# A one-token attention block on one core: the last eight rounds written out step by step, and one inverse root seeded on ScalarE

## The chip, the cores and the metric

One core of a Trainium2 chip runs the kernel. The time is device microseconds (us) of one execution. The runs of the kernel before gave 393.55, 395.03 and 395.13 us, median 395.03.

## What is computed

Four rows (batch B = 4, one token each, 512 channels) pass through an attention over a cache of 4096 positions and a small mixer. Both are modulated by six vectors that come from `c`.

```python
mod = (_silu(c) @ w_mod).reshape(c.shape[0], 6, 1, -1)
sa, ca, ga, sb, cb, gb = (mod[:, 0], mod[:, 1], mod[:, 2], mod[:, 3], mod[:, 4], mod[:, 5])
h = _layernorm(x, axis=-1) * (1 + ca) + sa
x = x + ga * _A_ref(h, A_k_cache, A_v_cache, A_wq, A_wo)
h = _layernorm(x, axis=-1) * (1 + cb) + sb
x = x + gb * _B_ref(h, B_w1, B_b1, B_w2, B_b2)
...
        scores = jnp.einsum("bhqd,bhkd->bhqk", q, k) * (Dh ** -0.5)
        p = _softmax(scores, axis=-1)
        o = jnp.einsum("bhqk,bhkd->bhqd", p, v)
        return (lambda x, *d: x.transpose(*d))(o, 0, 2, 1, 3).reshape(B, Sq, Hq * Dh) @ wo
...
        u = jnp.einsum("bsd,sf->bdf", h, w1) + b1                  # (B, D, F)
        u = _gelu(u)
        y = jnp.einsum("bdf,fs->bds", u, w2) + b2                  # (B, D, S)
```

There are 32 query heads on 8 key/value heads of 128 channels, and F = 1792. The two caches are 64 loads of 2 MB of float32 each, and every byte of them is read once.

## The kernel before

The work is 32 **rounds**: round i is batch row i // 8 and key/value head i % 8. Below, K29 is the keys of round 29 and V29 its values, 2 MB each. Up to round 29 the keys of round i + 2 and the values of round i come in one 4 MB load (`load_pair`); the last loads are cut: K30, K31, V28, V29 in two pieces, V30 in two, V31 in four (1 MB, 512 KB, 256 KB, 256 KB, called V31a to V31d here), and then `wm5`, the last 1 MB of `w_mod`. All loads land in one ring of three 4 MB slots (tag "kv"), are issued on SP's queue in program order, and a load can be issued when the reads of its slot's former content are over.

The steps of a round i, with their engines:

- `scores(i)`: eight products of the query with K on PE into a PSUM tile s; then the row maximum m on DVE (L241).
- `colmax(i)`: PE turns m (tile pm, L247), DVE takes the maximum over four groups (L249).
- `expo(i)`: PE spreads the maximum over the partitions (pb, L256), DVE copies it (L258), ACT makes the exponentials p and their sums l (L261).
- `transposes(i)`: PE turns p (eight blocks, L268, written over s) and sums l (pl, L272); DVE copies the blocks (L276) and forms the scaled selector sel (L279, L281).
- `values(i)`: sixteen products with V on PE (pv, L292; for round 30 the tile is called pve), then a copy on DVE (po, L296). Round 31 has `values_last` (L302, L306).
- `project_a(i)` picks the heads (pt, PE L317) and copies them (oT, DVE L319); `project_b(i)` multiplies with `wo` (pa, or pq and pgx in the last batch row, PE L328 and L335) and adds up on DVE (L344). Rounds 30 and 31 add straight in PSUM, in pgx; `wo` of these two rounds is first multiplied by the gate, by `fold_gate` (L537).

Once a batch row has its eight rounds, a `Mixer` does the second half for it in pieces between the rounds of the next row: residual, layernorm, modulation, second layernorm, and then seven pairs of expand (DVE, L405), gelu (ACT, L448) and contract (PE, L410). Batch row 3 has nothing after it: `finish` does its second half alone at the end. There and in `adaln` the inverse root of a variance is made on DVE from an integer seed and two refining steps (`rsqrt`, L99 to L116).

The order on each engine is the order of the calls; `manual_schedule` is on and nothing is rearranged. Until round 27 one loop body is repeated (L548 to L588), in which each helper holds steps of several engines: `scores` stands whole ahead of `project_a`, `transposes`, `project_b`, `colmax`, `values`, `expo`. Rounds 28 to 31 are written out below it (L589 to L639). The PSUM tiles pm, pb, pl, pt, pq and pst share two buffers, so each of them waits until the last but one has been read.

Of the kernel before, what the change touches and what calls it, by code (L numbers as in the profile page):

```python
# [28 lines left out]


@with_exitstack
def adaln_decode(ctx: ExitStack, tc: tile.TileContext, small, x, wmod, wq, kk, kv, vv, wo, out):
# [20 lines left out]
    nc.sync.dma_start(sm, small)  # L53
# [177 lines left out]
    S, SEL, SP = {}, {}, {}  # L231

    def scores(i):
        b, h = divmod(i, HKV)
        s = ps_s.tile([P, 1024], F32, name=f"s{i}", tag="s")
        for n in range(2):
            for c in range(4):
                mm(s[32 * c:32 * c + 32, n * 512:(n + 1) * 512], QT[:, b, h, :],  # L238
                   KT[i][:, (n * 4 + c) * 512:(n * 4 + c + 1) * 512], start=True, stop=True)
# [12 lines left out]

    def expo(i):
        s, mx = S[i]
        pb = ps_m.tile([P, 1], F32, name="pb", tag="m")
        mm(pb, mx.rearrange("o c r -> o (c r)"), neg1, start=True, stop=True)  # L256
        nm = wk.tile([P, 1], F32, name="nm")
        dv.tensor_copy(nm, pb)  # L258
        p = wk.tile([P, 1024], F32, name="p", tag="p")
        l = wk.tile([P, 1], F32, name="l")  # L260
        nc.scalar.activation(p, s, AF.Exp, bias=nm, accum_out=l)  # L261
        S[i] = [s, p, l]

    def transposes(i, then=None):
        s, p, l = S.pop(i)
        pt = s.rearrange("p (k n) -> p k n", k=8)
        for k in range(8):
            nc.tensor.transpose(pt[:, k, :], p[:, k * P:(k + 1) * P], ident)  # L268
        if then:
            then()  # L270
        pl = ps_m.tile([P, 1], F32, name="pl", tag="m")
        mm(pl, grp, l, start=True, stop=True)  # L272
        if i == NS - 1:
            dv.tensor_copy(pTl[:, :, :, 0:REP], pt.rearrange("p k (c r) -> p k c r", c=4)[:, :, :, 0:REP])
        else:
            dv.tensor_copy(pTs[i % 3][:, :, 0:2 * REP].rearrange("p k (c r) -> p k c r", c=2),  # L276
                           pt.rearrange("p k (h c r) -> p (k h) c r", h=2, c=2)[:, :, :, 0:REP])
        rl = wk.tile([P, 1], F32, name="rl")
        dv.reciprocal(rl, pl)  # L279
# [4 lines left out]
    PV = {}  # L284

    def values(i, ks, pv=None):
        if ks[0] == 0:
            PV[i] = ps_v.tile([P, 2 * DH], F32, name="pv", tag="pv") if pv is None else pv
        pv = PV[i]
        for k in ks:  # L290
            q = k % 4
            mm(pv[32 * q:32 * q + 32, :], pTs[i % 3][:, k, :],  # L292
               VT[i][:, k * 2:(k + 1) * 2, :].rearrange("p j d -> p (j d)"), start=(k < 4), stop=(k >= 12))
        if ks[-1] == 15:
            po = wk.tile([P, 2 * DH], F32, name="po")
            dv.tensor_copy(po, pv)  # L296
            SP[i] = (SEL.pop(i), po)

    def values_last(i, ks, pv):
        for k in ks:  # L300
# [3 lines left out]
        if ks[-1] == 7:  # L304
            po = wk.tile([P, DH], F32, name="po")
            dv.tensor_copy(po, pv)  # L306
            SP[i] = (SEL.pop(i), po)

    ACC = {}
    OT = {}  # L310

    def project_a(i):
        sel, po = SP.pop(i)
        pt = ps_m.tile([P, REP], F32, name="pt", tag="m")
# [3 lines left out]
        oT = wk.tile([P, REP], F32, name="oT")  # L318
        dv.tensor_copy(oT, pt)  # L319
        OT[i] = oT  # L320

    def project_b(i, pa=None):
# [7 lines left out]
        else:  # L330
# [54 lines left out]

    def bcast(h1, b, pb=None):
# [7 lines left out]
    def affine(pst, pb):  # L394
# [5 lines left out]
        rsqrt(var, P, "e", out=wr, times=w1n)  # L400
# [18 lines left out]
    class Mixer:  # L419
# [254 lines left out]
```

## Time and profile before

| | |
|---|---|
| median of three runs | 395.03 us |
| profiled execution | 393.89 us, span 392.1 us, granted TensorE clock 0.908 |
| PE busy | 298.3 us (76%), 3180 instructions |
| DVE busy | 180.3 us (46%), 491 instructions |
| ACT busy | 99.6 us (25%), 123 instructions, among them 22 table loads of 1283 ns |
| SP's DMA queue | 157.33 MB, 93.6% of 16 engines' span |
| HBM | 401 GB/s over the span |

The span is the stretch from the first to the last instruction of the profiled execution; the other 1.8 us of its 393.89 lie around it. In the views, a row of the timeline gives start and duration in us, engine, line of the kernel, operation, tiles and count; the bracket says how long the engine was idle just before, and who released it. A float32 product shows as two MATMUL records. PEld is the weight load that goes with a product, SPq and DVEq are the queues ahead of SP and DVE.

### The profile page before, as it was taken

The numbers are of one execution on the slowest core, as the hardware profiler recorded it, in microseconds if no ns is written. First come the engines' busy times: TensorE is split into PE (matmuls) and PEld (weight loads), VectorE is DVE, ScalarE is ACT, GpSimd is POOL, SyncE is SP. The second block draws the span as 40 slices with busy tenths as digits, with TensorE's granted clock in tenths as the row PEclk, the third lists the DMA queues.
The fourth block names the chain that finished last, engine by engine and source line by source line (L and its number), as shares of the span: only waits on it lengthen the run. The fifth ranks groups of instructions, "written<-read, shape, count | busy, mean of one in ns | idle before, by whom it ended". The sixth has DMA issues, their size and how long they took to land.

```text
span 392.1 us, 7228 instructions
## 1 busy us (share of the span) xinstructions
PE 298.3 (76%) x3180; PEld 146.8 (37%) x3180; DVE 180.3 (46%) x491; ACT 99.6 (25%) x123; POOL 0.7 (0%) x6
## 2 busy tenths in 40 slices
PE   0578685913868739978698879998888879899885
PEld 0012142400533305434243325553334225555663
DVE  0620331510433404666365524765555356557766
ACT  1001120110110201114548111145751111465316
POOL 0000000000000000000000000000000000000000
PEclk9989886985998957999899976999999889999997
DMA  8999999999999999999999999999999999999600
GB/s 325 428 431 431 428 453 440 404 448 431 425 431 426 436 426 438 433 440 439 426 431 424 430 435 430 433 428 434 436 435 430 431 430 430 416 425 420 258 3 3
DMA packets 7415, 157.80 MB, mean 402 GB/s; under 512 B 964, under 2 KB 980, under 8 KB 1368
## 3 DMA queue, kind: packets, MB, share of 16 engines
q1 hardware_dynamic: 7376, 157.33, 93.6%
q8 instruction: 25, 0.41, 0.4%
q14 instruction: 6, 0.05, 0.0%
q10 hardware_dynamic: 8, 0.00, 0.0%
HBM read 157.32 MB, written 0.01 MB: 401 GB/s over the span
## 4 chain that ended last, share of the span: by engine, by line
DMA 64%; PE 27%; DVE 6%; ACT 1%; issue 1%; SPq 0%; DVEq 0%
DMA kv<-in_kv 57%; PE s L238 7%; DMA kv<-in_vv 5%; PE pv L292 3%; PE pa L328 3%; PE s L268 3%; PE s L137 2%; PE qs L152 2%; DMA sm<-in_small 2%; PE pt L317 2%; DVE mx L249 1%; PE py L410 1%; DVE acc L344 1%; PE pb L256 1%; PE pm L223 1%
## 5 line engine op out<-in xcount | busy, mean ns | idle before, releaser
L238 PE MATMUL s<-kv,QT 128*32 128x512 f32 x512 | 76.5, 725 | 55.0 <-DMA kv<-in_kv 54.6
L261 ACT ACTIVATE p<-s,nm 128x1024 f32<-128x1024 f32 x32 | 35.7, 1115 | 212.9 <-DVE nm L258 212.8
L241 DVE TENSOR_REDUCE m<-s 128x1 f32<-128x1024 f32 x32 | 39.2, 1225 | 104.9 <-PE s L238 104.8
L292 PE MATMUL pv<-kv,pT 128*32 128x256 f32 x960 | 64.5, 387 | 0.0
L238 PEld LDWEIGHTS s<-kv,QT 128*32 128x32 f32 x512 | 15.6, 123 | 94.8 <-DMA kv<-in_kv 62.4
L268 PE MATMUL s<-ident,p 128*128 128x128 f32 x256 | 36.5, 288 | 0.6 <-ACT p L261 0.6
L268 PEld LDWEIGHTS s<-ident,p 128*128 128x128 f32 x256 | 31.5, 157 | 3.7 <-ACT p L261 1.9
L292 PEld LDWEIGHTS pv<-kv,pT 128*32 128x32 f32 x960 | 25.6, 110 | 15.3 <-issue 0.6
L317 PEld LDWEIGHTS pt<-sel,po 128*128 128x128 f32 x126 | 17.6, 202 | 30.8 <-issue 25.7
L328 PE MATMUL pa<-wo,oT 128*32 128x512 f32 x192 | 27.3, 642 | 0.0
L249 DVE TENSOR_REDUCE mx<-pm 1x128 f32<-1x512 f32 x32 | 21.5, 672 | 0.7 <-PE pm L247 0.7
L317 PE MATMUL pt<-sel,po 128*128 128x4 f32 x126 | 20.3, 266 | 1.1 <-DVE po L296 1.0
L448 ACT ACTIVATE u<-u 128x1024 f32<-128x1024 f32 x20 | 20.3, 1051 | 2.2 <-DVE u L405 2.1
L405 DVE TENSOR_SCALAR u<-hb,wr,sm 128x512 f32<-128x512 f32 x40 | 19.9, 540 | 1.9 <-PE py L416 1.9
L137 PE MATMUL s<-wm,sT 128*4 128x512 f32 x16 | 9.6, 770 | 14.3 <-DVE sT L123 14.3
L344 DVE TENSOR_TENSOR acc<-acc,pa 128x512 f32<-128x512 f32 x21 | 14.5, 688 | 11.3 <-PE pa L328 11.3
L296 DVE COPY po<-pv 128x256 f32<-128x256 f32 x30 | 12.7, 423 | 11.8 <-PE pv L292 11.8
L261 ACT ACT_TABLE_LOAD x9 | 11.5, 1283 | 25.6 <-DVE nm L258 25.5
L256 PEld LDWEIGHTS pb<-neg,mx 1*128 1x128 f32 x64 | 9.4, 182 | 20.0 <-DVE mx L249 20.0
L256 PE MATMUL pb<-neg,mx 1*128 1x1 f32 x64 | 12.1, 256 | 5.9 <-DVE mx L249 5.9
L448 ACT ACT_TABLE_LOAD x11 | 14.1, 1283 | 0.2
L276 DVE COPY pT<-s 128x128 f32<-128x128 f32 x31 | 9.0, 291 | 9.9 <-PE s L268 9.2
(142 smaller groups left out, 231.1 us busy)
## 6 DMA issues: line engine op xcount, KB each, us to landing
kv<-in_kv SPq DMA_DIRECT2D x28, 4096.0 KB, 21.6
wq<-in_wq SPq DMA_DIRECT2D x2, 4096.0 KB, 16.3
wo<-in_wo SPq DMA_DIRECT2D x4, 2048.0 KB
kv<-in_kv SPq DMA_DIRECT2D x3, 2048.0 KB, 17.4
wm<-in_wmod SPq DMA_DIRECT2D x2, 2048.0 KB, 16.1
kv<-in_kk SPq DMA_DIRECT2D x1, 4096.0 KB
kv<-in_vv SPq DMA_DIRECT2D x3, 1024.0 KB
kv<-in_kv SPq DMA_DIRECT2D x2, 1024.0 KB, 17.6
```

Of the source, the lines that this page charges most:

```text
L238: mm(s[32 * c:32 * c + 32, n * 512:(n + 1) * 512], QT[:, b, h, :], KT[i][:, (n * 4 + c) * 512:(n * 4 + c + 1) * 512], start=True, stop=True)
L241: dv.tensor_reduce(m, s, axis=AX.X, op=OP.max)
L249: dv.tensor_reduce(mx, pm.rearrange("o (c r) -> o r c", c=4).unsqueeze(1).to_broadcast([1, 4, 32, 4]), axis=AX.X, op=OP.max)
L256: mm(pb, mx.rearrange("o c r -> o (c r)"), neg1, start=True, stop=True)
L261: nc.scalar.activation(p, s, AF.Exp, bias=nm, accum_out=l)
L268: nc.tensor.transpose(pt[:, k, :], p[:, k * P:(k + 1) * P], ident)
L292: mm(pv[32 * q:32 * q + 32, :], pTs[i % 3][:, k, :], VT[i][:, k * 2:(k + 1) * 2, :].rearrange("p j d -> p (j d)"), start=(k < 4), stop=(k ...
L317: mm(pt, po[:, c * DH:(c + 1) * DH], sel[:, c * REP:(c + 1) * REP], start=(c == 0), stop=(c == n - 1))
L328: mm(pa[32 * g:32 * g + 32, :], oT[:, g:g + 1].to_broadcast([P, 32]), wo_t[h][:, g, :], start=True, stop=True)
L344: dv.tensor_add(ACC[b], ACC[b], pa)
L405: dv.tensor_scalar(u[:, e, :], hb, wr[:, j:j + 1], b1[:, j:j + 1], op0=OP.mult, op1=OP.add)
L448: nc.scalar.activation(u, u, AF.Gelu_apprx_tanh)
```

## The change

Three things change.

1. **The helpers are split** into steps of one engine each (`scores`, `row_max`, `turn_max`, `col_max`, `spread_max`, `copy_max`, `expo`, `turn`, `sums`, `copy_p`, `scale`, `copy_v`, `pick`, `copy_o`, `project`, `add_up`; the mixer's `fold`, `gather`, `spread` likewise). The loop runs to round 23 in the old order. From the end of round 23 on a string lists the steps one by one, so that values can go in quarters and a step of one engine no longer brings the other engines' steps with it. V29 comes in one load and not in two.
2. **The last batch row's first inverse root** is seeded on ACT (`Abs_reciprocal_sqrt`) and refined once on DVE. Two small activations (T2, T3) load the table for it and then the gelu table again. The sign of the modulated row is turned by this, which `w1` in place of `w1n` takes back.
3. **The load of `small`** (128 rows of 236 bytes: w1, b1, w2, c, b2) is cut into rows 0 to 5, 6 to 15 and 16 to 127.

```diff
-    nc.sync.dma_start(sm, small)
+    for lo, hi in ((0, 6), (6, 16), (16, P)):
+        nc.sync.dma_start(sm[lo:hi], small[lo:hi])
...
+    def adaln_last(b, pst):
+        mean, var = norm(pst)
...
+        nc.scalar.activation(y, var, AF.Abs_reciprocal_sqrt, scale=1.0 / C2)
+        dv.scalar_tensor_tensor(a, XK[:, b], mean, prep[:, 3], op0=OP.subtract, op1=OP.mult)
+        dv.scalar_tensor_tensor(t, y, var, y, op0=OP.mult, op1=OP.mult)
+        dv.scalar_tensor_tensor(y, t, 3.0 * C2, y, op0=OP.subtract, op1=OP.mult)
+        dv.scalar_tensor_tensor(h1, a, y, prep[:, 2], op0=OP.mult, op1=OP.subtract)
+        return h1, stats(h1, b)
...
-    for i in range(NS - 4):
+    for i in range(NS - HKV):
...
-    load_v(t[:, 1], n + 1, (0, 16, 32))
-    project_a(n - 1)
-    project_b(n - 1)
-    scores(n + 2)
-    transposes(n + 1)
...
-    finish(B - 1, pgx[:, 0], x3, mix)
+    cuts = {NS - 1: (0, 16, 24, 28, 32), NS - 2: (0, 16, 32)}
+    last = [(0, 1, 2, 3), (4, 5), (6,), (7,)]
+    PLAN = """
...
+    p29 v31.0 V30 f x v31.1 a30 A30 v31.2 P29 v31.3 V31 p30 a31 E A31 I p31 zs c g T2 zg c zx zm T3 c c zg zb
+    zn zw0 zc zw1
+    """
...
+        elif step == "T2":
+            nc.scalar.activation(tab, neg1, AF.Abs_reciprocal_sqrt)
+        elif step == "T3":
+            nc.scalar.activation(tab, neg1, AF.Gelu_apprx_tanh)
...
+    finish(B - 1, pgx[:, 0], py[:, 0], row.hb, row.wr)
```

In the two quoted lines of the string, v31.0 to v31.3 are the four parts of the values of round 31 (V31a to V31d), p is `project`, a `pick`, A its copy, P `add_up`, V the copy of the values, x, g and c the expand, gelu and contract of one pair of the mixer of row 2, f one gate product, E and I the residual of row 3, and the steps with z belong to the second half of row 3 (zs statistics, zg gather, zx copy of x, zm modulation, zb spread, zn second norm, zw0 and zw1 the product with `wm5`, zc the close of row 2's mixer).

What stands on the engines, at three places. First PE, from the scores of round 29 on (tile s29, the first product that needs the last whole pair of loads; py is the mixer's contract, pt the pick, pq the project, pv the values of round 27). Before:

```order
L238 MATMUL s29_2526<-kv_2413,QT_116 32x512 x8
L317 MATMUL pt_2537<-sel_2340,po_2515 128x4 x2
L268 MATMUL s28_2415<-ident_98,p_2481 128x128 x8
L272 MATMUL pl_2550<-l_2482,grp_114 128x1
L335 MATMUL pq_2557<-wo2_129,oT_2540 32x128 x16
L247 MATMUL pm_2575<-ident_98,m_2535 1x128
L292 MATMUL pv_2579<-kv_2413,pT0_120 32x256 x8
L256 MATMUL pb_2588<-neg1_87,mx_2577 128x1
L292 MATMUL pv_2579<-kv_2413,pT0_120 32x256 x8
L410 MATMUL py_2609<-u_2517,sm_88 32x128 x8
L317 MATMUL pt_2625<-sel_2444,po_2607 128x4 x2
L335 MATMUL pq_2630<-wo2_129,oT_2628 32x128 x16
```

The same place of the changed kernel:

```order
L437 MATMUL py_2517<-u_2426,sm_88 32x128 x8
L280 MATMUL pl_2527<-l_2457,grp_116 128x1
L327 MATMUL pt_2539<-sel_2485,po_2531 128x4 x2
L437 MATMUL py_2517<-u_2460,sm_88 32x128 x8
L241 MATMUL s29_2551<-kv_2463,QT_118 32x512 x8
L276 MATMUL s28_2432<-ident_100,p_2536 128x128 x8
L305 MATMUL pv_2572<-kv_2463,pT0_122 32x256 x4
L250 MATMUL pm_2582<-ident_100,m_2580 1x128
L305 MATMUL pv_2572<-kv_2463,pT0_122 32x256 x8
L261 MATMUL pb_2594<-neg1_87,mx_2592 128x1
L280 MATMUL pl_2599<-l_2537,grp_116 128x1
L241 MATMUL s30_2602<-kv_2479,QT_118 32x512 x8
```

The pick of round 26 and two contracts of the mixer now stand ahead of s29, the projects of rounds 26 and 27 have moved behind, and s30 follows ahead of the last quarter of the values of round 27.

Second PE, at the end of the attention (pve is the tile of the values of rounds 30 and 31, pgx the sum of the last two projects). Before, from the second half of the values of round 30 on:

```order
L292 MATMUL pve_2837<-kv_2766,pT0_120 32x256 x8
L317 MATMUL pt_2885<-sel_2728,po_2882 128x4 x2
L302 MATMUL pve_2837<-kv_2766,pTl_126 32x128 x16
L335 MATMUL pgx_2884<-wo6_131,oT_2888 32x128 x16
L302 MATMUL pve_2837<-kv_2766,pTl_126 32x128 x16
L636 MATMUL pgx_2884<-ep_2890,ident_98 128x128
L317 MATMUL pt_2946<-sel_2787,po_2943 128x4
L335 MATMUL pgx_2884<-wo6_131,oT_2948 32x128 x16
```

The changed kernel, from its last three quarters of the values of round 30 on:

```order
L305 MATMUL pve_2819<-kv_2753,pT0_122 32x256 x12
L347 MATMUL pq_2864<-wo4_132,oT_2862 32x128 x16
L312 MATMUL pve_2819<-kv_2753,pTl_128 32x128 x24
L327 MATMUL pt_2910<-sel_2816,po_2897 128x4 x2
L312 MATMUL pve_2819<-kv_2753,pTl_128 32x128 x8
L347 MATMUL pgx_2861<-wo6_133,oT_2913 32x128 x16
L327 MATMUL pt_2942<-sel_2849,po_2924 128x4
L678 MATMUL pgx_2861<-ep_2944,ident_100 128x128
L347 MATMUL pgx_2861<-wo6_133,oT_2947 32x128 x16
```

The values of round 31 no longer wait behind the pick of round 30, and the project of round 30 stands behind all of them; the product with ep has moved behind the last pick.

Third DVE, in the modulation of batch row 3, from the aggregate of its statistics on. Before:

```order
L374 BN_AGGR mv_3011<-pst_2972 128x2
L103 TENSOR_SCALAR ye_3015<-mv_3011 128x1
L381 SCALAR_TENSOR_TENSOR a_3013<-xk_232,mv_3011,prep_132 128x128
L106 SCALAR_TENSOR_TENSOR te_3016<-ye_3015,mv_3011 128x1
L107 SCALAR_TENSOR_TENSOR ye_3015<-te_3016,ye_3015 128x1
L108 SCALAR_TENSOR_TENSOR te_3016<-ye_3015,mv_3011 128x1
L111 SCALAR_TENSOR_TENSOR qe_3017<-te_3016 128x1
L115 SCALAR_TENSOR_TENSOR ye_3015<-qe_3017,ye_3015 128x1
L383 SCALAR_TENSOR_TENSOR h1_3014<-a_3013,ye_3015,prep_132 128x128
```

The changed kernel:

```order
L388 BN_AGGR mv_2992<-pst_2980 128x2
L407 SCALAR_TENSOR_TENSOR a_2996<-xk_234,mv_2992,prep_134 128x128
L408 SCALAR_TENSOR_TENSOR te_2995<-ye_2994,mv_2992 128x1
L409 SCALAR_TENSOR_TENSOR ye_2994<-te_2995,ye_2994 128x1
L410 SCALAR_TENSOR_TENSOR h1_2997<-a_2996,ye_2994,prep_134 128x128
```

Four small operations have left DVE there; te now reads a seed that ACT writes (L406 of the changed kernel) while DVE makes a.

More of the change, by code (lines that the diff above doesn't have):

```diff
@@ L264, in transposes, with spread_max, copy_max @@
-    def transposes(i, then=None):
-        s, p, l = S.pop(i)
-        pt = s.rearrange("p (k n) -> p k n", k=8)
+        M[i] = mx
+    def spread_max(i):
+        pb = ps_m.tile([P, 1], F32, name="pb", tag="m")
+        mm(pb, M[i].rearrange("o c r -> o (c r)"), neg1, start=True, stop=True)
+        M[i] = pb
+    def copy_max(i):
+        nm = wk.tile([P, 1], F32, name="nm")
+        dv.tensor_copy(nm, M[i])
+        M[i] = nm
+    def expo(i):
+        PL[i] = p, l = wk.tile([P, 1024], F32, name="p", tag="p"), wk.tile([P, 1], F32, name="l")
+        nc.scalar.activation(p, S[i], AF.Exp, bias=M.pop(i), accum_out=l)
@@ L303, in values_last, with copy_v, pick @@
                    start=(k == 0), stop=(k == 7))
[L304 to L314, printed above, removed]
+    def copy_v(i):
+        pv = PV[i]
+        PV[i] = wk.tile(list(pv.shape), F32, name="po")
+        dv.tensor_copy(PV[i], pv)
+    ACC, OT = {}, {}
+    def pick(i):
+        po, sel = PV.pop(i), SEL.pop(i)
+        OT[i] = pt = ps_m.tile([P, REP], F32, name="pt", tag="m")
         n = po.shape[-1] // DH
@@ L561, in adaln_decode @@
         scores(i + 2)
+        row_max(i + 2)
         if i:
-            project_a(i - 1)
-        transposes(i + 1)
+            pick(i - 1)
+            copy_o(i - 1)
+        turn(i + 1)
+        sums(i + 1)
+        copy_p(i + 1)
+        scale(i + 1)
         if i:
-            project_b(i - 1)
-        colmax(i + 2)
+            project(i - 1)
+            add_up(i - 1)
+        turn_max(i + 2)
+        col_max(i + 2)
         values(i, range(8))
+        spread_max(i + 2)
+        copy_max(i + 2)
         expo(i + 2)
@@ L626, in adaln_decode @@
-    x3 = pgx[:, 4]
-    project_a(n + 2)
-    ep = cst.tile([P, P], F32, name="ep")
-    residual(ep, ACC.pop(B - 1))
-    fold_gate(gate, (6, 7))
-    pvl = pve[:, 1, 0:DH]
-    values_last(n + 3, range(0, 4), pvl)
-    project_b(n + 2, x3)
-    for ks in ((4, 5), (6,), (7,)):
-        values_last(n + 3, ks, pvl)
-    mm(x3, ident, ep, start=False, stop=False)
-    project_a(n + 3)
-    project_b(n + 3, x3)
-    finish(B - 1, pgx[:, 0], x3, mix)
+    mix, row = Mixer(B - 2), Mixer(B - 1)
+    pve = pgx = ep = spare = slot = None
@@ new lines, in adaln_decode @@
+    e29 v27.3 f f t29 S30 g C29 L28 V27 LT p26 P26 LV28 m30 s31 X30 a27 LV29 A27 b30 p27 B30 S31 c v28.0
+    P27 l29 v28.1 v28.2 L29 e30 m31 v28.3 V28 t30 X31 a28 LT A28 b31 p28 x B31 v29.0 f LV30 C30 v29.1 x
+    e31 v29.2 g l30 v29.3 LV31 L30 g v30.0 P28 V29 t31 f LW l31 a29 v30.1 L31 v30.2 g C31 v30.3 Y A29
+    p29 v31.0 V30 f x v31.1 a30 A30 v31.2 P29 v31.3 V31 p30 a31 E A31 I p31 zs c g T2 zg c zx zm T3 c c zg zb
+    zn zw0 zc zw1
+    """
+    TABLE = {"s": scores, "S": row_max, "m": turn_max, "X": col_max, "b": spread_max, "B": copy_max, "e": expo,
+             "t": turn, "l": sums, "C": copy_p, "L": scale, "V": copy_v, "a": pick, "A": copy_o, "P": add_up,
+             "LP": load_pair}
```

222 lines of the change are left out of this document (116 added, 106 removed).

## The prediction

> **What bounds the kernel now.** I read the page's 40 slices first, then the chain of waits, the landings of the last loads, and the timeline of the last 55 us.
>
> ```profile
> DMA  8999999999999999999999999999999999999600
> GB/s 325 428 431 431 428 453 440 404 448 431 425 431 426 436 426 438 433 440 439 426 431 424 430 435 430 433 428 434 436 435 430 431 430 430 416 425 420 258 3 3
> ```
>
> A slice is 9.8 us. The loads run at 404 to 453 GB/s from the second slice to the 37th and end in the 38th, near 370 us; nothing in the change alters the bytes. About 22 us of arithmetic follow. So a gain can only come from how long after the last load the work ends. The chain of waits puts the seam at 368.3 us:
>
> ```profile
> 349.60 18.68 DMA kv<-in_vv
> 368.28 0.02 issue
> 368.31 0.05 DVEq L405
> 368.41 1.00 DVE kv L405 x2
> ```
>
> Taken alone this says that a load held DVE until 368.3. The timeline says otherwise:
>
> ```profile
> 366.88 1.08 PE L335 MATMUL pq<-wo,oT 128*32 128x128 f32 x32 [0.42 <-DVE oT L319]
> 368.03 0.29 DVE L344 TENSOR_TENSOR acc<-acc,pq 128x128 f32<-128x128 f32 x1 [1.20 <-PE pq L335]
> ```
>
> DVE was busy with the sum of round 29 until 368.32, and this waited for PE. The load landed at the same moment by chance. What ends last at this place is PE's own order, so I look at when the last loads landed and when PE took them:
>
> ```profile
> 349.60 0.33 SPq L218 DMA_DIRECT2D kv<-in_vv  x1
> kv<-in_vv SPq DMA_DIRECT2D x1, 256.0 KB, 19.0
> 356.93 0.33 SPq L206 DMA_DIRECT2D kv<-in_wmod  x1
> kv<-in_wmod SPq DMA_DIRECT2D x1, 1024.0 KB, 14.7
> ```
>
> V31c landed at 349.60 + 19.0 = 368.6, wm5 at 356.93 + 14.7 = 371.6. Between the two lie V31d (256 KB) and wm5 (1024 KB), 3.0 us for 1280 KB; V31d's fifth of it puts its landing at **369.2** (an estimate; certain is only 368.6 to 371.6). PE's side:
>
> ```profile
> 339.94 1.92 PE L238 MATMUL s<-kv,QT 128*32 128x512 f32 x16 [1.08 <-DMA kv<-in_kv]
> ...
> 369.79 0.61 PE L317 MATMUL pt<-sel,po 128*128 128x4 f32 x4 [0.97 <-DVE po L296]
> ...
> 372.10 1.06 PE L302 MATMUL pve<-kv,pTl 128*32 128x128 f32 x32
> ...
> 373.23 0.29 DVE L306 COPY po<-pve 128x128 f32<-128x128 f32 x1 [0.90 <-PE pve L302]
> ...
> 373.57 0.39 PE L317 MATMUL pt<-sel,po 128*128 128x4 f32 x2
> ...
> 374.21 1.08 PE L335 MATMUL pgx<-wo,oT 128*32 128x128 f32 x32 [0.25 <-DVE oT L319]
> ...
> 375.36 0.30 DVE L361 BATCH_NORM_STATS2 st<-pgx 128x6 f32<-128x128 f32 x1 [1.20 <-PE pgx L335]
> ```
>
> At 339.94 PE starts s29 the moment K29 is there, after 1.08 us without work. After that no row of PE names a DMA. It ends the values of round 31 at 373.16, four microseconds after V31d. **PE is late against the loads**, and this is what a better order can take.
>
> **The order of the last rounds.** How much must PE do?
>
> ```profile
> 339.94:375.33 35.39, 32.27 (x554) 21.67 (x555) 21.57 (x57) 16.14 (x18) 0.00 (x0) 1.00 0.82 344
> 346.79 0.62 PE L410 MATMUL py<-u,sm 128*32 128x128 f32 x16
> ```
>
> From s29 to the end of the last project PE is busy 32.27 us of 35.39, so it idles 3.1 us. The changed order does the pick of round 26 (0.6, as in the row of 369.79, 0.4 of it not overlapped) and two contracts (0.4 each beside neighbours, 0.62 alone) ahead of s29, into the idle 1.08 us. This leaves 32.27 - 1.2 = 31.1 us. Without any idle the last project would end at 339.94 + 31.1 = 371.0.
>
> The other floor is V31d. Its four products are a quarter of the sixteen in the row of 372.10, 0.3 us, and a result shows some 0.2 us later: 369.7. In the old order the path from there to the statistics takes 375.36 - 373.16 = 2.2 us (copy, pick, copy, project). In the new one the project of round 30 stands between the values and the last pick. A project holds PE 0.8 us (32 records of the row of 366.88 less its drain), from 369.45 to 370.25, where the pick would have started at 370.1; that adds 0.2. DVE has the two operations of E there, 0.6 us from 370.05, over before the pick's result at 370.65. The statistics then start at 369.7 + 2.2 + 0.2 = 372.1.
>
> The landing floor, 372.1, is the later one, and PE has about 1 us in hand against it. Whether the loads in between let PE get there, I checked along the new order with these prices and two more:
>
> ```profile
> 351.23 1.09 PE L268 MATMUL s<-ident,p 128*128 128x128 f32 x8
> ...
> 357.63 1.07 PE L292 MATMUL pv<-kv,pT 128*32 128x256 f32 x16
> ```
>
> A turn holds PE 0.85 (less its drain), a quarter of the values 0.5, scores 1.9, pm, pb and pl 0.2 to 0.3 each. The landings, counted back from V31c at 430 GB/s (2 MB in 4.9 us), are K30 344.8, K31 349.7, V28 354.6, V29 359.4, V30 364.3, V31a 366.8, V31b 368.0. From 339.94: s29, turn 28, three quarters of V27 and three small steps end at 345.0; s30, a quarter, turn 29, a project and pm at 349.2; s31 from 349.7, a pick, a project, pb and a contract at 353.5; V28 from 354.6, three small steps, turn 30, a pick and a project at 359.4; V29, a quarter of V30, turn 31, two pl, a pick, the rest of V30 and a project at 366.0. From there PE waits for V31a, b, c and d in turn. No load is late for more than 1.1 us, and at the end PE is ahead. So I take 372.1: **375.36 - 372.1 = 3.3 us**. If V31d lands at 371.6 the gain is 0.9; if PE makes up only half of its lateness, 1.6. With V31d as early as V31c, at 368.6, it would be 3.9.
>
> V30 and V31 now wait for the last quarter of the values of round 27, which stands behind s30, hence behind K30. That quarter ends at 345.0 + 1.9 + 0.5 = 347.4. K31, V28 and V29 have then still to land, to 359.4, so the queue runs dry only if the quarter slips by some 10 us. V29 in one piece costs nothing: its first quarter is due at 359.4, when it lands.
>
> **The inverse root of the last row.** All of it lies on the path.
>
> ```profile
> 376.37 0.27 DVE L374 BATCH_NORM_AGGREGATE mv<-pst 128x2 f32<-128x24 f32 x1 [0.29 <-PE pst L369]
> ...
> 376.74 0.34 DVE L381 SCALAR_TENSOR_TENSOR a<-xk,mv,prep 128x128 f32<-128x128 f32 x1
> 377.00 0.21 DVE L106 SCALAR_TENSOR_TENSOR te<-ye,mv 128x1 f32<-128x1 f32 x1
> 377.25 0.16 DVE L107 SCALAR_TENSOR_TENSOR ye<-te,ye 128x1 f32<-128x1 f32 x1
> ...
> 378.09 0.35 DVE L383 SCALAR_TENSOR_TENSOR h<-a,ye,prep 128x128 f32<-128x128 f32 x1
> 359.05 0.16 DVE L258 COPY nm<-pb 128x1 f32<-128x1 f32 x1 [0.55 <-PE pb L256]
> ...
> 359.31 1.11 ACT L261 ACTIVATE p<-s,nm 128x1024 f32<-128x1024 f32 x1 [3.57 <-DVE nm L258]
> 8.78 0.22 ACT L119 ACTIVATE sg<-sm 128x16 f32<-128x16 f32 x1 [6.76 <-DMA sm<-in_small]
> ```
>
> From mv's end, 376.64, to h: 1.45 us. New: 0.1 to ACT (nm ends at 359.21, p starts at 359.31), 0.22 for a small activation, some 0.05 back, that is 377.01, while DVE makes a until 377.01 as well. Then te and ye, with gaps 0.25 and 0.2, and h at 377.5. This saves 0.6; with a slower hand-over, less. No row shows this function; the nearest, sg, differs in width alone. Bounds: 0.3 to 0.7. I take **0.55**.
>
> The tables: a load is 1.28 us, and the activation behind it starts at once. ACT is free for them:
>
> ```profile
> 360.53 1.28 ACT L448 ACT_TABLE_LOAD   x1
> ...
> 361.82 2.01 ACT L448 ACTIVATE u<-u 128x1024 f32<-128x1024 f32 x2
> ...
> 380.46 0.69 ACT L399 ACTIVATE hb<-py,mv 128x512 f32<-128x512 f32 x1 [9.96 <-PE py L391]
> ```
>
> T2 goes into the 9.96 us ahead of hb, T3 between the seed (over at about 373.7 in the new time) and hb (380.46 - 3.8 = 376.7); 1.28 + 0.2 end at 375.2. Cost nothing; if the cover were gone, 1.5 us for one of the two.
>
> **The close of row 2's mixer** moves on DVE from a gap to just ahead of the last twelve expands.
>
> ```profile
> 378.90 0.34 DVE L468 TENSOR_SCALAR zk<-py,sm 128x128 f32<-128x128 f32 x1
> ...
> 381.18 5.56 DVE L405 TENSOR_SCALAR uu<-hb,wr,sm 128x512 f32<-128x512 f32 x12
> ...
> 382.61 5.35 ACT L512 ACTIVATE uu<-uu 128x1024 f32<-128x1024 f32 x6
> ```
>
> The first pair of expands (0.93) would be ready at 382.1 and is asked for at 382.61; 0.34 later it is still in time, and each next pair is made in 0.93 and used in 0.95. Between 0 and 0.34; I take 0.1.
>
> **The load of small** stands second in the queue and lands at 8.78 (row of sg); the pieces add two issues of 0.4 us on SP while 2 MB of wm01 are still coming in. The second and third slices of the page, full at 428 and 431 GB/s, show that the stream does not hang on the start. Bounds: 0.2 us sooner or later at the first products, hidden at the end. I take 0.
>
> **Sum**: 3.3 + 0.55 - 0.1 = 3.75 us, 393.89 - 3.75 = 390.1 for an execution like the profiled one. The median of the runs is 1.14 above it, so against the median 395.03 - 3.75 = **391.3**.
>
> **The rivals.**
>
> *The loads end the work later* (V31d lands toward 371.6): nothing speaks for exactly a fifth, since the engines end unevenly (258 GB/s in the 38th slice). Gain 0.9 to 2.5 instead of 3.3; the middle gives 395.03 - 1.7 - 0.45 = 392.9, the end 393.7.
>
> *PE does not catch up.* Small waits for DVE grow, since turn, spread, pick and project share two buffers and DVE carries 21.57 of the 35.39 us. Half the gain: 395.03 - 1.6 - 0.45 = 393.0. Against it speaks the 1 us in hand.
>
> *The root gains nothing*, because ACT's hand-over takes what three operations of DVE took: 391.8, inside the range.
>
> *Slower: half clock at the end.* PE now waits for V31b, c and d, and a wait may drop its clock.
>
> ```profile
> 309.38 3.43 PE L238 MATMUL s<-kv,QT 128*32 128x512 f32 x16 [1.61 <-DMA kv<-in_kv]
> 290.08 1.92 PE L238 MATMUL s<-kv,QT 128*32 128x512 f32 x16 [1.60 <-DMA kv<-in_kv]
> ```
>
> Two waits of 1.6 us, one followed by scores at nearly half speed, one not. Were the clock halved from V31b through the second norm of the last row, PE's path there (values 0.9, two projects 1.9, pick 0.4, ep 0.4, two gathers 0.8, spread 1.1, and 1.0 of contracts that no longer hide) would double: 6.5 - 3.75 = 2.75 lost, 397.8. It decides from a wait of about 1.6 us on; along the new order no wait there is over 0.8 us. [...]
>
> **How the numbers follow.** Forecast 0.58, loads later 0.14, PE not catching up 0.18, half clock for the whole stretch 0.06; 0.04 for half clock over a part of it, about 394. The low end is the forecast with 3.9, 0.7 and no cost for the close, 390.4, less 0.8 for a median nearer to the profiled run: 389.6. The high end takes in the later loads and part of the half clock: 394.5. A measurement tells half a per cent, 2.0 us, from no change. Faster than 393.05: all of the forecast, half of the two middle rivals, 0.74; slower than 397.0: 0.06; within: 0.20.
>
> **What would show it.** Right: s29 with its transposes next, PE rows that name a DMA at the values of round 31, the statistics at 372 to 372.5, h about 0.85 us after mv's end, ACT's two loads ended before hb. Wrong: statistics after 373.5 with PE waiting for DVE (PE not catching up), or for a DMA (loads later), or a granted clock of 0.5 after 366.

## The result and the profile after

| | before | after |
|---|---|---|
| median, side by side on one chip | 393.68 us (5 runs, 393.55 to 395.13) | 391.57 us (5 runs, 390.91 to 392.77) |
| profiled execution | 393.89 us, span 392.1 us | 391.15 us, span 389.0 us |
| ACT table loads | 22 | 24 |

The ratio is 0.9936, with a 95% interval of 0.9908 to 0.9965: the changed kernel is faster by 0.35 to 0.92 per cent. By the two spans it gains 3.1 us.

First the page of the changed kernel, the row of the 40 slices with the rate of the loads:

```profile
GB/s 327 431 431 431 423 438 433 422 436 431 426 435 431 433 430 431 430 435 433 434 435 427 436 428 440 436 438 430 431 430 433 431 433 430 411 425 419 366 22 3
```

The loads run as before. The last of them end at the seam of the 38th and 39th slices (a slice is 9.7 us here), so near 370 us as before. What changed is what comes behind them. The chain of waits of the changed kernel (start, us, engine or queue, tile and line) shows where it stops hanging on them:

```profile
297.15 22.94 DMA kv<-in_kv
320.23 1.08 PE pv L305 x8
```

The last load in this chain landed at 320.09; the values of round 25 wait for it and start at 320.23. From there to hb (the spread row that ACT writes for the last expands) at 377.14 the chain holds PE and, for short steps, DVE; no later load is in it. The timeline and the windows (length, then busy time of PE, PEld, DVE, ACT and POOL, PE's granted clock, DMA share, GB/s) tell the same:

```profile
320.23 1.08 PE L305 MATMUL pv<-kv,pT 128*32 128x256 f32 x8 [3.77 <-DMA kv<-in_kv]
...
322.19 3.64 PE L241 MATMUL s<-kv,QT 128*32 128x512 f32 x16
...
341.18 1.90 PE L241 MATMUL s<-kv,QT 128*32 128x512 f32 x16
...
366.71 1.06 PE L312 MATMUL pve<-kv,pTl 128*32 128x128 f32 x32
...
367.83 0.42 DVE L318 COPY po<-pve 128x256 f32<-128x256 f32 x1 [2.96 <-PE pve L312]
...
368.31 0.64 PE L312 MATMUL pve<-kv,pTl 128*32 128x128 f32 x16 [0.55 <-DVE po L318]
...
369.42 0.64 PE L312 MATMUL pve<-kv,pTl 128*32 128x128 f32 x16
...
371.55 1.08 PE L347 MATMUL pgx<-wo,oT 128*32 128x128 f32 x32
...
372.69 0.30 DVE L375 BATCH_NORM_STATS2 st<-pgx 128x6 f32<-128x128 f32 x1 [1.20 <-PE pgx L347]
```

```profile
341.18:372.66 31.48, 30.93 (x533) 20.23 (x528) 19.34 (x53) 14.02 (x16) 0.00 (x0) 1.00 0.88 371
320.00:328.00 8.00, 7.77 (x76) 3.73 (x80) 2.09 (x4) 0.18 (x2) 0.00 (x0) 0.57 1.01 438
```

Three things are to be seen. The statistics of the last row start at 372.69 instead of 375.36. PE is busy for 30.93 of the 31.48 us from s29 on, and the one gap, 0.55 us at 368.31, is a wait for DVE, not for a load. And s29 itself starts at 341.18, 1.24 us later than before: PE waited 3.77 us for the values of round 25 and then ran at a granted clock of 0.57 up to 328 us (the products of s27 took 3.64 us, at full clock 1.92). Half clock is not new there: before, s26 took 3.43 us (the row of 309.38 in the prediction), and s27 took 3.23 us:

```profile
320.62 3.23 PE L238 MATMUL s<-kv,QT 128*32 128x512 f32 x16 [2.09 <-DMA kv<-in_kv]
```

The last row's norm and root, from the timeline of the changed kernel (mv is the pair of mean and variance, ye the seed, h the modulated row):

```profile
373.76 0.27 DVE L388 BATCH_NORM_AGGREGATE mv<-pst 128x2 f32<-128x24 f32 x1 [0.35 <-PE pst L383]
...
374.06 0.20 ACT L406 ACTIVATE ye<-mv 128x1 f32<-128x1 f32 x1 [1.69 <-DVE mv L388]
...
374.29 1.28 ACT L682 ACT_TABLE_LOAD   x1
...
374.77 0.35 DVE L410 SCALAR_TENSOR_TENSOR h<-a,ye,prep 128x128 f32<-128x128 f32 x1
...
377.14 0.69 ACT L426 ACTIVATE hb<-py,mv 128x512 f32<-128x512 f32 x1 [1.36 <-PE py L418]
```

From mv's end (374.03) to h it is 0.74 us, where it was 1.45. ACT takes the seed 0.03 us after mv's end, and the table for gelu is back at 375.57, 1.57 us ahead of hb. So the span's gain is: statistics 2.67, root 0.71, less 0.28 that is given back in small steps (0.06 from the statistics to mv, 0.06 from hb to the last two sums, 0.16 behind the last store's issue): 3.10.

### The profile page after: what moved, and what is told of

Same layout as the page of the kernel before. It is cut to its first block, busy times and chain, and to the rows that moved or that the text cites. A ratio compares the mean times of both kernels' runs of the same rounds, so it can differ in the third digit from the quotient of the medians.

```text
span 389.0 us, 7235 instructions
## 1 busy us (share of the span) xinstructions
PE 299.8 (77%) x3180; PEld 149.0 (38%) x3180; DVE 179.4 (46%) x487; ACT 102.6 (26%) x128; POOL 0.7 (0%) x6
## 4 chain that ended last, share of the span: by engine, by line
DMA 53%; PE 37%; DVE 6%; ACT 1%; issue 1%; SPq 0%; DVEq 0%
DMA kv<-in_kv 51%; PE s L241 9%; PE pv L305 5%; PE s L276 4%; PE pa L340 3%; PE pt L327 3%; PE s L140 2%; PE qs L155 2%; DMA sm<-in_small 2%; DVE mx L255 2%; PE pq L347 2%; PE py L437 1%; PE pb L261 1%; DVE acc L358 1%; PE pm L226 1%
## 5 line engine op out<-in xcount | busy, mean ns | idle before, releaser
L305 PE MATMUL pv<-kv,pT 128*32 128x256 f32 x960 | 65.9, 389 | 3.8 <-DMA kv<-in_kv 3.8
L276 PE MATMUL s<-ident,p 128*128 128x128 f32 x256 | 37.3, 293 | 0.0
L250 PEld LDWEIGHTS pm<-ident,m 128*1 128x1 f32 x32 | 2.5, 79 | 29.9 <-DVE sel L295 17.2
```

The costliest lines, as they stand in the source:

```text
L276: nc.tensor.transpose(pt[:, k, :], PL[i][0][:, k * P:(k + 1) * P], ident)
L305: mm(PV[i][32 * q:32 * q + 32, :], pTs[i % len(pTs)][:, k, :], VT[i][:, k * 2:(k + 1) * 2, :].rearrange("p j d -> p (j d)"), start=(k < 4) ...
```

## The experiments

The theory was: the order gains what it does because PE no longer comes late to the last loads, and it falls short of 3.3 us because of two things that the changed kernel does to itself, the half clock after the wait at 320.23 and the wait for the copy at 368.31. The rivals were that the last loads hold the end, that the gain comes from the root or from the cut of `small`, and that the loads moved. "The changed kernel" is the one after the change; times are medians, the ratio is to the kernel before on the same chip.

### One part alone

`order_only` is the changed kernel with the old root:

```diff
-            self.h1, self.st = (adaln if self.b < B - 1 else adaln_last)(self.b, self.st)
+            self.h1, self.st = adaln(self.b, self.st)
...
-            self.hb, self.wr = affine(self.st, self.pb, w1n if self.b < B - 1 else w1)
+            self.hb, self.wr = affine(self.st, self.pb, w1n)
...
-    ... zs c g T2 zg c zx zm T3 c c zg zb
+    ... zs c g zg c zx zm c c zg zb
```

> The changed kernel with the integer seed and two refining steps on DVE back in the last row, and without the two table activations; order and loads stay as changed. Theory 1 (the root lies on the path): the start of h comes 1.45 us after the end of mv instead of 0.74, the time is 0.7 us above the changed kernel's 391.57, about 392.3, ratio to the kernel before 0.9955 to 0.9965. Rival (the root is hidden, the whole gain is the order's): 391.6, ratio 0.994. In both the statistics of the last row start where they do in the changed kernel, 372.7 give or take 0.5.

`root_only` is the kernel before with the new root (`adaln_last`, `times=w1`, and the two table loads in `finish`, ahead of the statistics and behind h).

> The kernel before with the new root alone: seed on ACT, one refining step, two table activations. Theory 1: h starts 0.74 us after mv, 0.7 us gained, ratio 0.998. Rival (a table load delays hb, or the seed's hand-over eats the gain): ratio 1.000 or above, and ACT's row of hb starts right behind a table load.

`one_small` is the changed kernel with `small` in one load:

```diff
-    for lo, hi in ((0, 6), (6, 16), (16, P)):
-        nc.sync.dma_start(sm[lo:hi], small[lo:hi])
+    nc.sync.dma_start(sm, small)
```

> The changed kernel with the load of small in one piece again. Theory 1 (engine order, the loads run as before): no change against the changed kernel, ratio 0.992 to 0.995, all loads land at the same times within 0.5 us. Rival (the cut shifts which completion a later load waits for, or eases some DMA engines, and so the last loads land earlier): ratio 0.996 or above, the last loads issued later by some us.

| | median | ratio, interval | span |
|---|---|---|---|
| order_only | 391.41 us | 0.9926 (0.9896 to 0.9955) | 389.6 us |
| root_only | 393.38 us | 0.9974 (0.9944 to 1.0004) | 391.2 us |
| one_small | 390.76 us | 0.9896 (0.9846 to 0.9946) | 388.7 us |

The order alone has nearly all of the gain, and the root alone can't be told from no change. For `order_only` the median came out as the rival had it, not as theory 1 did, but its interval just reaches both, and it is of another chip than the 391.57. The cut of `small` gains nothing that can be measured: without it the statistics start at 372.58, and the median is even the lower one, again on another chip. The cut does move something: in the changed kernel ACT's first table load stands behind the landing of `small`, at 9.03 us instead of 0.74, and sg, the first activation, starts at 10.32 instead of 8.68. The first products start 0.4 us later by it (14.56 and 14.18), and nothing of this is seen at the end.

With the old root inside the new order, the timeline gives

```profile
373.73 0.27 DVE L388 BATCH_NORM_AGGREGATE mv<-pst 128x2 f32<-128x24 f32 x1 [0.35 <-PE pst L383]
...
375.45 0.35 DVE L397 SCALAR_TENSOR_TENSOR h<-a,ye,prep 128x128 f32<-128x128 f32 x1
...
377.82 0.69 ACT L426 ACTIVATE hb<-py,mv 128x512 f32<-128x512 f32 x1 [6.99 <-PE py L418]
```

that is 1.45 us from mv's end to h, and hb 0.68 us later than in the changed kernel: there the root is worth 0.7 us of path in the traces. The medians of the two (391.41 and 391.57) don't show it. In the old order, `root_only`, it is not:

```profile
376.84 0.35 DVE L397 SCALAR_TENSOR_TENSOR h<-a,ye,prep 128x128 f32<-128x128 f32 x1
...
377.27 0.62 PE L424 MATMUL py<-kv,sm 128*32 128x128 f32 x16
...
378.59 0.27 DVE L375 BATCH_NORM_AGGREGATE mv<-pst 128x2 f32<-128x24 f32 x1 [0.28 <-PE pst L370]
```

h comes 0.71 us sooner after the first mv than before, but from h to the second mv, the row of 378.59, it is 1.75 us where it was 1.39: PE is still at the contracts of row 2's mixer (L424) until 377.89, and the gather of the second norm stands behind them. Half of the gain goes into this wait. The changed order has moved one contract and the modulation product away from there; with it h to the second mv is 1.40 us with the new root, and so root and order add up.

### What held the kernel before

`before_no_v31` leaves out the load of the values of round 31 and reads those of round 30 in their place.

```diff
-    load_v(t[:, 1], n + 3, (0, 16, 24, 28, 32))
+    VT[n + 3] = VT[n + 2]
```

> The kernel before without the load of the values of round 31 (2 MB, the last before wm5): its products read the values of round 30 instead, so this part of the result is left out. Theory 1 (PE is late, the load holds nothing): the same end within 0.4 us, values of round 31 at 370.3 as before, ratio 0.999 to 1.001. Rival (the chain of waits is right, the last loads hold the end): 2 to 4 us earlier, ratio 0.990 to 0.995.

It took 393.85 us, ratio 0.9992 (0.9956 to 1.0028). Its timeline:

```profile
339.56 1.92 PE L238 MATMUL s<-kv,QT 128*32 128x512 f32 x16 [1.27 <-DMA kv<-in_kv]
...
374.97 0.30 DVE L361 BATCH_NORM_STATS2 st<-pgx 128x6 f32<-128x128 f32 x1 [1.20 <-PE pgx L335]
```

From s29 to the statistics it is 35.41 us with the last load gone, and 35.42 with it. The chain of waits of before put a load of 18.68 us there; taking the load away changes nothing that the time or the trace shows. At its end the kernel before was held by PE and its order. Nor did the loads move much: the one for round 27's scores and round 25's values landed some 0.4 us sooner in the changed kernel (its first products start at 320.23, before at 320.62), and since from s29 on no load held the kernel before, this can't be the gain.

### What holds the changed kernel

Four kernels; `after_again` and `after_third` are the changed kernel once more, each on the chip of the kernels that were run with it. `after_no_v31` is the same cut in the changed kernel (its values of round 31 are those of round 30). `warm` puts six unused products of 512 columns into PE's wait ahead of the first values of round 25:

```diff
-    ... R G b26 V24 C25 v25.0 M B26 e26
+    ... R G b26 V24 C25 W v25.0 M B26 e26
...
+        elif step == "W":
+            d = ps_m.tile([P, D], F32, name="warm", tag="m")
+            for _ in range(6):
+                mm(d, ident, prep.rearrange("p a n -> p (a n)"), start=True, stop=True)
```

`own_pv` gives the values of round 31 a PSUM tile of their own, so that they need not wait for the copy of round 30; `warm_own_pv` has both.

```diff
-                values_last(i, last[q], pve[:, 1, 0:DH])
+                if q == 0:
+                    pvl = ps_v.tile([P, DH], F32, name="pvl", tag="pv")
+                values_last(i, last[q], pvl)
```

> The changed kernel with six products of 128x512 that nobody reads, put on PE into its 3.8 us wait for V25, to keep the clock up; nothing else changes. Theory 1 (that wait drops the clock for 7 us, PE is 1.2 us late from there to the end, and PE's lateness sets the end): scores of round 27 take 1.9 us instead of 3.6, those of round 29 start at 339.9 to 340.3 instead of 341.1, the statistics start 0.3 to 0.7 us earlier, where the landing of the last values stops them. Rival (the end is set by the landing of the last values alone): scores of round 29 earlier, the statistics where they are, within 0.15. Other rival (the clock does not follow the wait): the scores of round 27 stay at 3.6.

> The changed kernel with the values of round 31 in a PSUM tile of their own (that of the other rounds, which is free by then) instead of the second half of pve. Theory 1 (the copy of round 30 waits for products of round 31, and those for the copy, only because they share the tile): the 2.96 us wait of that copy and the 0.55 us of PE go, the statistics start 0.2 to 0.5 us earlier, no more because the last piece lands at about 369.2. Rival (the last landing is the bound): no change, and PE's rows of round 31 name a DMA.

> Both edits. Theory 1: statistics at 371.9 to 372.2, 0.5 to 0.8 us earlier than in the changed kernel, PE waiting for the last pieces by then. Rival: each gain is the same lateness taken twice, so both together give no more than the better of the two.

> The changed kernel itself, as the reference on the same chip as the three others. About 390.8 to 391.6, statistics of the last row at 372.6 to 372.7, scores of round 29 at 341.1, the first products with V25 after 3.5 to 3.8 us of waiting and the scores of round 27 at half clock, as in all three profiles of this order so far.

> Changed kernel without the load of round 31's values; its products read round 30's values in place. Theory 1 (behind the last load stands work on TensorE that is late by itself): the statistics come 0 to 0.8 us earlier, counted from the landing of round 28's keys, since TensorE has nearly no free time from there. Rival (the changed kernel is held by the loads alone): 2 us earlier or more.

> The changed kernel on the same chip, as the reference for the other kernels of this call: 6.0 us from the first products of round 31 to the statistics, 1.45 us from h to the second mean and variance at most 1.40, the time between 390.8 and 392.5 us.

| | median | ratio, interval | span | s29 to statistics |
|---|---|---|---|---|
| changed kernel, first | 391.57 us | 0.9936 (0.9908 to 0.9965) | 389.0 us | 31.51 us |
| after_again | 392.35 us | 0.9911 (0.9878 to 0.9944) | 390.3 us | 33.97 us |
| after_third | 391.47 us | 0.9922 (0.9892 to 0.9952) | 389.4 us | 32.29 us |
| after_no_v31 | 391.36 us | 0.9920 (0.9890 to 0.9951) | 388.9 us | 31.52 us |
| warm | 392.20 us | 0.9923 (0.9893 to 0.9954) | 388.7 us | 32.67 us |
| own_pv | 391.16 us | 0.9896 (0.9861 to 0.9932) | 389.0 us | 32.51 us |
| warm_own_pv | 391.07 us | 0.9894 (0.9860 to 0.9927) | 390.4 us | 30.88 us |

No time is told apart from another here. The traces are. First `after_no_v31`:

```profile
341.06 1.90 PE L241 MATMUL s<-kv,QT 128*32 128x512 f32 x16
...
368.20 0.64 PE L312 MATMUL pve<-kv,pTl 128*32 128x128 f32 x16 [0.55 <-DVE po L318]
...
372.58 0.30 DVE L375 BATCH_NORM_STATS2 st<-pgx 128x6 f32<-128x128 f32 x1 [1.21 <-PE pgx L347]
```

Without the last load it has the same 0.55 us wait and the same 31.5 us from s29 on. So in the first profile of the changed kernel the last load holds nothing either. But it is close behind. `warm` takes PE's lateness away:

```profile
316.67 5.42 PE L673 MATMUL warm<-prep,ident 128*128 128x512 f32 x12
...
323.12 1.92 PE L241 MATMUL s<-kv,QT 128*32 128x512 f32 x16
...
339.76 1.90 PE L241 MATMUL s<-kv,QT 128*32 128x512 f32 x16
...
354.05 0.64 PE L305 MATMUL pv<-kv,pT 128*32 128x256 f32 x8 [0.29 <-DMA kv<-in_kv]
...
366.42 1.08 PE L312 MATMUL pve<-kv,pTl 128*32 128x128 f32 x32 [0.25 <-DMA kv<-in_vv]
...
372.43 0.30 DVE L375 BATCH_NORM_STATS2 st<-pgx 128x6 f32<-128x128 f32 x1 [1.20 <-PE pgx L347]
```

s27 runs at full clock (1.92 us), s29 starts 1.42 us sooner, and then the values of round 28 and of round 31 have to wait for their loads: only 0.26 us of it arrive at the statistics, just under the 0.3 to 0.7 that were expected. This compares one execution of each kernel; the profiled one of `warm` (390.83 us) is the fastest of its eight. Work and loads are within a microsecond of each other, and whichever is later in an execution holds the end. In `after_third` the loads were the later ones (K26 was there at 310.07, not at 309.15):

```profile
366.93 1.08 PE L312 MATMUL pve<-kv,pTl 128*32 128x128 f32 x32 [0.25 <-DMA kv<-in_vv]
...
368.74 0.65 PE L312 MATMUL pve<-kv,pTl 128*32 128x128 f32 x16 [0.73 <-DMA kv<-in_vv]
```

and in `after_again` later still (310.67): there the values of round 28 waited 0.78 us for their load, those of round 29 0.67 and the first of round 31 0.26, and the statistics came at 373.98 instead of the 372.6 to 372.7 that were expected. These shifts of up to 1.5 us between executions of one kernel are larger than anything that was left to gain, and the medians of the table can't tell such gains apart.

The wait for the copy is real, though. `own_pv`, whose loads were as late as those of `after_third`:

```profile
365.92 0.42 DVE L318 COPY po<-pve 128x256 f32<-128x256 f32 x1 [1.22 <-PE pve L305]
...
367.08 1.08 PE L312 MATMUL pvl<-kv,pTl 128*32 128x128 f32 x32 [0.35 <-DMA kv<-in_vv]
...
368.41 0.64 PE L312 MATMUL pvl<-kv,pTl 128*32 128x128 f32 x16 [0.25 <-DMA kv<-in_vv]
...
372.76 0.30 DVE L375 BATCH_NORM_STATS2 st<-pgx 128x6 f32<-128x128 f32 x1 [1.21 <-PE pgx L347]
```

The copy of round 30 now starts right after round 30's own products, at 365.92 instead of 367.83, and from the first products of round 31 to the statistics it is 5.68 us (5.98 in the changed kernel, 6.16 in `after_third`). In the profiled execution of `warm_own_pv` s26 ran at half clock (3.53 us), s29 came at 343.22 and the statistics at 374.10, so it can't say whether the two gains add up. But as PE was late there, no product of round 31 waited for a load:

```profile
368.76 1.64 PE L312 MATMUL pvl<-kv,pTl 128*32 128x128 f32 x48
```

From there to the statistics PE is never idle, and it is 5.34 us. Against the 5.98 of the changed kernel, which waited for no load there either, the shared tile costs 0.64 us when the loads are there; in `own_pv` the wait for a load took half of this.

### An order that should have been shorter

`early_project` has round 31 in a tile of its own, and the pick and the project of round 30 ahead of the last pieces of the values of round 31:

```diff
-    p29 v31.0 V30 f x v31.1 a30 A30 v31.2 P29 v31.3 V31 p30 a31 E A31 I p31 zs
+    p29 v31.0 V30 f x a30 A30 v31.1 p30 P29 E v31.2 v31.3 V31 a31 A31 I p31 zs
```

> Changed kernel with a tile of its own for round 31's values, the pick of round 30 ahead of the second piece of round 31's products, and the projection of round 30 ahead of the third and fourth pieces; the last pick stands directly behind the copy of round 31. Theory 1 (what stands on TensorE between the landing of the last loads and the last projection sets the end): 5.2 to 5.4 us from the first products of round 31 to the statistics, 0.3 to 0.5 below the kernel with the tile alone (5.68) and 0.6 to 0.8 below the changed kernel (6.0), and the time 0.6 to 0.9 us below the changed kernel's on the same chip. Rival (the landing of the last piece holds the end): the products of the third and fourth pieces wait for a DMA, the path stays at 5.6 us or more and the time does not move.

It took 390.76 us, ratio 0.9909 (0.9880 to 0.9938), which is not told from `after_third` on the same chip. Both theories missed. The timeline:

```profile
366.72 1.06 PE L312 MATMUL pvl<-kv,pTl 128*32 128x128 f32 x32
...
370.62 0.38 PE L327 MATMUL pt<-sel,po 128*128 128x4 f32 x2 [0.41 <-DVE po L318]
...
372.41 0.30 DVE L375 BATCH_NORM_STATS2 st<-pgx 128x6 f32<-128x128 f32 x1 [1.20 <-PE pgx L347]
```

The path is 5.69 us, as in `own_pv`, but no product waits for a load. The same work stands on PE between the first products of round 31 and the statistics, and now nothing covers the copy of round 31's values: PE waits 0.41 us for it. In the changed order the project of round 30 lies there, and with a tile of its own and the loads landed that order needs 5.34 us. The new order is no shorter: it makes a wait for DVE of its own.

### The root in the old order, with PE cleared

`root_free_pe` is `root_only` with everything of row 2's mixer and of the modulation product that stood on PE between the statistics and the second spread moved behind that spread:

```diff
-        modmm(pg, 5, (0,))
-        mix.consume()
         h1, stm = adaln_last(b, pst)
...
-        mix.close()
...
-        modmm(pg, 5, (1, 2, 3))
+        modmm(pg, 5)
+        mix.consume()
...
+        mix.close()
```

> Kernel before with the new root, and with the modulation products, the contracts and the close of row 2's mixer moved behind the second spread of the last row's norm on TensorE, so that nothing stands ahead of it. Theory 1 (the root alone kept 0.36 of its 0.71 us because those contracts stand ahead of the second gather): from h to the second mean and variance 1.39 to 1.40 us instead of 1.75, and hb 0.71 us earlier than in the kernel before counted from s29, so 0.36 earlier than with the root alone. Rival (the second gather waits for something else, or the contracts delay the last row's own contracts by as much): 1.75 us stays, or hb is earlier and the end is not.

It took 398.70 us, ratio 1.0108 (1.0069 to 1.0146): slower than the kernel before. The timeline and the windows:

```profile
377.90 0.35 DVE L397 SCALAR_TENSOR_TENSOR h<-a,ye,prep 128x128 f32<-128x128 f32 x1
...
378.85 0.62 PE L370 MATMUL pst<-stm,ones 128*128 128x24 f32 x2 [1.68 <-DVE stm L364]
...
379.30 2.06 PE L405 MATMUL py<-h,ident 128*128 128x128 f32 x8
...
379.51 0.27 DVE L375 BATCH_NORM_AGGREGATE mv<-pst 128x2 f32<-128x24 f32 x1 [0.71 <-PE pst L370]
...
381.39 0.69 ACT L413 ACTIVATE hb<-py,mv 128x512 f32<-128x512 f32 x1 [2.49 <-PE py L405]
...
385.89 0.35 DVE L482 TENSOR_SCALAR zk<-py,sm 128x128 f32<-128x128 f32 x1 [4.81 <-PE py L424]
```

```profile
378.80:383.00 4.20, 4.15 (x44) 3.80 (x48) 1.40 (x8) 1.68 (x4) 0.00 (x0) 0.50 0.00 0
```

With nothing to do PE waits 1.68 us, its granted clock falls to 0.50, and the gather takes 0.62 us for 0.40, the spread 2.06 for 1.14. h to the second mv is 1.61 us; less the 0.22 of the slow gather it is 1.39, so the contracts were the cause of the 1.75, but the gain went into the clock: counted from s29, hb comes 0.75 us later than with the root alone, where 0.36 sooner was expected. The larger loss is one of this kernel's order: the close of row 2's mixer (zk) stands on DVE ahead of the expands, it waits for the moved contracts, and the expands start at 386.17, 4.78 us after hb (0.78 in the changed kernel).

## Why the prediction was right, and where it was not

**The time** came out at 391.57 us, 0.3 us from the 391.3. But it was reckoned from a median of before of 395.03, and side by side that median was 393.68; the gain is 2.1 us by the medians and 3.1 by the spans, where 3.75 stood in the sum. The base was 1.35 us too high and the gain by the medians 1.64 too large; that the two nearly cancel is luck. (`after_again` and `after_third`, each with its own median of before on its chip, gain 2.4 and 2.6 us.)

**PE was late against the loads, and the order takes this.** Right, and shown: without its last load the kernel before takes the same 35.4 us from s29 to the statistics, and the order alone gives 0.9926.

**The size, 3.3 us, was too large by 0.6** in the first profile, where the statistics gained 2.67 us and came 0.2 us behind the 372 to 372.5 that was to show the forecast right. The forecast took the larger of two floors: the landing of V31d, and PE's work without idle, which ended a whole microsecond earlier. The landing floor stands. V31d was issued at 351.75 and landed 17.2 us later, at 368.95, 0.25 earlier than estimated. Its products are the second half of the row of 369.42, so they start near 369.65, and from there to the statistics it is 3.0 us (2.9 in the sum): had PE been there in time, 372.0. The step that failed is PE's floor, "339.94 + 31.1 = 371.0". The work was right, 30.93 us. The start was not: s29 started at 341.18 (+1.24), and 0.55 us came in at the copy; 371.0 + 1.24 + 0.55 - 0.17 = 372.62, and the last project ends at 372.63. PE's "1 us in hand" was used up by these two.

- *The late start.* Before, PE waited 1.61 us ahead of s26 and 2.09 us ahead of s27; the new order makes 0.49 and 3.77 us of this. A pick now stands ahead of s26, s26 runs at full clock behind its shorter wait (1.92 us for 3.43), and so PE is done sooner with what stands ahead of the next load: the idle time comes in one piece. Behind it the granted clock from 320 to 328 us is 0.57 (0.79 before), and the first values of round 25 and a pick stand ahead of s27, which starts at 322.19 (320.62 before). So s29 was late. The forecast looked for half clock at the end of the kernel, not at the start of its own window. `warm` shows the clock as the cause (1.42 us sooner at s29), and also that repairing it alone brings 0.26, since the loads are then the later ones.
- *The copy.* Rounds 30 and 31 share the tile pve, so the copy of round 30 waits for the first products of round 31, and the second ones wait for the copy. The rows of order in the section on the change show the products one behind the other; the forecast did not ask what the copy between them waits for. With a tile of its own the path is 0.3 us shorter with late loads, 0.64 with none.

**The waits for V31a to d**, which were to follow "in turn", didn't come in the first profile; in `after_third` and `own_pv` two came (0.25 and 0.73, 0.35 and 0.25), in `warm` and `after_again` one. V28 didn't wait either (PE took it with no gap), for the same late s29.

**The root, 0.55 us**, measured 0.71: just above the upper bound. Of the 0.16, 0.07 is the hand-over to ACT, for which 0.1 was taken and which is 0.03 (374.03 to 374.06); 0.05 was taken off for a slow hand-over that didn't come, and the rest is rounding in the sum.

**The tables** cost nothing, as said: ACT idled for 1.36 us ahead of hb after the second of them (from 375.78 to 377.14).

**The close of row 2's mixer** costs nothing rather than 0.1: from ACT's first activations (377.87) to the next (379.29) it is 1.42 us, as before (1.43). The 0.28 us that was given back came in three pieces of 0.06 to 0.16, named above, and the runs don't show why.

**The cut of `small`** was put at nothing, and at the end it is nothing. That it would put a table load of 1.28 us behind the landing of `small` was not foreseen; it is hidden, and the second to fourth slices of the page run at 431 GB/s all the same.

**The rivals.** "PE does not catch up" is the one that had some truth: PE was the later one, but by 0.6 us instead of half the gain. "The loads later" holds the end in other executions: in `after_again` with rows of PE that name a load and the statistics at 373.98, behind the 373.5 that was to show it. "The root gains nothing" is refuted for the path of the new order (0.71 us); in the old one half of it went into a wait. Half clock over the stretch that the rival named didn't happen in the changed kernel, whose granted clock is 1.00 from s29 (341.18) to 380 us; it fell at 381.69, among the last contracts, as it fell at 384.75 in the kernel before; `root_free_pe` shows that it was a real danger, in another order. There the clock fell in a wait of 1.68 us, and gather and spread took 1.6 and 1.8 times as long. The forecast's condition, "a wait of about 1.6 us on", does not hold: in `warm_own_pv` s26 ran at half clock behind a wait of 0.47 us (the last section). So the short waits of the new order were no guarantee against this rival.

## What to carry to other kernels

When two limits lie within a microsecond, a change is worth only the distance to the next one: compute both floors, and ask of each what its first moment rests on, since an order that closes many small gaps may gather them into one large wait further up (here 1.61 and 2.09 us became 0.49 and 3.77). A PSUM tile that two steps share is a dependency that no order of calls shows (0.64 us here); look at what each copy waits for. And work that stands in front of a critical product may be what keeps the clock up (from 378.8 to 383.0 us it was 0.50 in `root_free_pe`, where that work was moved behind, and from 373 to 382 us 1.00 in `root_only`, where it stood): before you clear it, ask what the wait that remains does to the clock, and look at the granted clock afterwards.

## What the hardware showed that was not expected

**In these runs the length of a wait didn't decide the clock.** Scores after waits for keys, two rows from `root_free_pe` and then one from `warm_own_pv`:

```profile
309.96 3.48 PE L239 MATMUL s<-kv,QT 128*32 128x512 f32 x16 [1.70 <-DMA kv<-in_kv]
...
320.72 1.92 PE L239 MATMUL s<-kv,QT 128*32 128x512 f32 x16 [1.70 <-DMA kv<-in_kv]
...
311.15 3.53 PE L241 MATMUL s<-kv,QT 128*32 128x512 f32 x16 [0.47 <-DMA kv<-in_kv]
```

Two waits of 1.70 us in one execution, one with half speed behind it and one without, and half speed behind a wait of 0.47 us. What the changes of the clock have in common here is their distance. A short window whose granted clock (the number behind the five busy times) lies between 0.50 and 1.00 dates a change. For `warm_own_pv`:

```profile
311.00:311.10 0.10, 0.00 (x0) 0.00 (x0) 0.00 (x0) 0.00 (x0) 0.00 (x0) 0.58 0.76 328
314.40:314.60 0.20, 0.20 (x8) 0.10 (x4) 0.00 (x0) 0.00 (x0) 0.00 (x0) 0.93 1.90 819
```

The clock fell at 311.02 and rose at 314.43, 3.41 us later. Dated in the same way, it fell in the kernel before at 309.66, 319.90 and 384.75 and rose at 313.07, 323.31 and 388.16; in the changed kernel it fell at 320.25 and 381.69 and rose at 327.08 and 385.11. In `root_free_pe` the means of two windows (0.92 from 374.0 to 378.8 us, 0.82 from 383.0 to 388.0, with 0.50 between them) put a fall at about 378.0 and the rise behind it at about 384.8. These stretches of half speed lasted 3.41 us or, in the changed kernel and in `root_free_pe`, 6.8, and in the kernel before and in the changed kernel the distances between the dates are multiples of 3.41 us within 0.02 (384.75 - 309.66 is 22 times 3.413, 381.69 - 320.25 is 18 times 3.413). The runs don't show where this comes from. By the rows, PE had been without a product for 0.8 us when the clock fell at 378.0, and for 0.33 us at 311.02. How much idle time is enough, the runs don't settle.

**The loads shift between executions.** The scores of round 26, which start when their keys are there, began between 309.06 and 311.15 us in the ten profiles of the changed order, whose loads up to there bring the same bytes in the same order; in the three of the changed kernel itself at 309.15, 310.07 and 310.67. The runs don't show where it comes from.
